# Gated mix of two Fourier filters: the hand-written order list in another arrangement

## Chip, cores and metric

The kernel runs on one core of a Trainium2 chip. The metric is the device time of one execution in microseconds, as the median of the runs. The engines are PE (matmul), DVE (vector), ACT (scalar), POOL (GpSimd) and SP, which issues nearly all transfers.

## The reference

```python
def filt(x, w_r, w_i):                                # x: (1, 2048, 1024) bf16
    X = rfft2(x.astype(float32), axes=(-2, -1)) * (w_r + 1j * w_i)
    return irfft2(X, s=(2048, 1024), axes=(-2, -1)).astype(bfloat16)

x = A_x
g = sigmoid((x * gate_w).sum(-1, keepdims=True))      # one gate value per row
out = g * filt(x, A_w_r, A_w_i) + (1 - g) * filt(x, B_w_r, B_w_i)
```

`B_x` isn't used. Both filters act on the same x, so the forward transform is done once; the two products with the weights and the two inverse transforms share most of their work, and the gate enters where the last step along the rows mixes the two halves.

## The kernel before

The transforms are matmuls with constant matrices (DFT factors). The 2048 rows are taken as 16 x 128 (index s = 0 to 15 for the factor of 16), and the 1024 columns are folded into even and odd frequencies. No loop orders the work: every step is a short code in one long string, `ORDER`, and the codes are called one after the other. A code's fields are its indices, then a PSUM bank (the last digit, for matmul codes) or an engine letter (A = ACT, D = DVE, P = POOL, S = SP). Each engine runs its own instructions strictly in the order in which the list names them, and waits, by semaphores that the framework derives from the tiles, for what others must have finished. So the list decides three things: the order on each engine and on SP's transfer queue, which engine does a copy or a sum, and which PSUM bank a matmul writes (a bank is free again when its reader has copied it out).

The codes that the texts below speak of, with the lines that the profile shows (copies by ACT and DVE all go through one helper, line 201 or 203):

| code | what it does | engine, line |
|---|---|---|
| `x:S:s:n`, `c:S:name`, `W:S:n` | load n slices of x, a constant, the weights of unit n | SP, L249, L254/L261, L273 |
| `F1:s:e`, `F1:s:o` | first matmul stage, even or odd part of slice s (8 matmuls) | PE, L336 |
| `FC`, `FX` | copy one half, or all, of an F1 result from PSUM to SBUF | ACT or DVE |
| `FD`, `FP` | fold it: a sum and a difference | DVE or POOL, L422 |
| `neg`, `pw` | prepare constants for F3 and for the patch | POOL |
| `F2:n:t`, `F3:n` | second and third stage for unit n (0 to 7 even frequencies, 8 to 15 odd) | PE, L528, L569 |
| `T:n:t`, `X:n` | copies of their results | ACT or DVE |
| `P:n` | product of X with the weights, 128 x 4096 | DVE, L586 |
| `Y:n`, `NA:n`, `N:n` | patch of the first column for even units | PE, DVE, POOL |
| `GH`, `GC`, `Gt`, `GK`, `GZ`, `GS` | gate values: matmuls, copies, sigmoid | PE, ACT, DVE |
| `GA:b`, `GB:b` | gate folded into the constants EA and EB, four slices from b | POOL or DVE, L515, L519 |
| `J:n`, `R:n:t` | first inverse stage of unit n (32 matmuls), and its two evictions | PE L632; ACT or DVE |
| `H:n:t` | store an eviction to a scratch tensor in DRAM (256 KB) | SP, L654 |
| `L:0:v`, `L:1:v` | read back row pair v, even or odd half (512 KB) | SP, L665 |
| `V:h:v:s`, `VC` | inverse along the 128 rows, row s of pair v, with EA and EB; its copy | PE, L675; ACT or DVE |
| `C:h:v:s`, `U:1:v:s` | last inverse stage, folded (4 matmuls of 256 columns) or full (4 of 512) | PE, L712, L703 |
| `E`, `EX`, `EQ`, `ES`, `EF` | even part: copies, then sum and difference, kept in SBUF as EV | ACT, DVE, POOL |
| `Ks`, `Kf`, `OK`, `QD`, `QP`, `OC`, `OP`, `OR` | odd part added to and subtracted from EV | ACT, DVE, POOL |
| `S:S:v` | store row pair v of the output | SP, L862 |

The stages overlap. In the profiled execution, F1 runs from 4.6 to 20 us, units 1 to 15 follow each other until 77 us on F2, F3, P, J and R, the even read-backs and V:0, C:0 run beside them from 57 us on, and the odd half V:1, C:1, U:1 and the output are last. A read-back of a half can be issued only when every store of that half has landed, since each pair holds rows of all units. The odd stores end with `H:15:0`; behind it on SP's queue stand `L:0:3` and the eight `L:1:v`.

Buffers: eight PSUM banks; two T, X and V tiles each, three product tiles, five eviction tiles that the output tiles share; eight slots of temporaries in `wx`, which also holds the weights of units 8 to 11.

```python
    def gate_a(e, b):
        s = slice(int(b), int(b) + 4)
        Q[e].tensor_tensor(C["EA"][:, s], C["EA"][:, s], bc(C["E"][:]).to_broadcast([P, 4, 128]), ALU.mult)
    ...
    order = [tok.split(":") for tok in ORDER.split()]
    for t in order:
        fn[t[0]](*t[1:])
```

Of the kernel before, what the change touches and what calls it, by code (L numbers as in the profile page):

```python
# [21 lines left out]


ORDER = """
warm:8 c:A:F1 x:S:0:1 x:S:1:1 F1:0:o:0 F1:0:e:4 F1:1:e:5 c:A:gws x:S:2:2 F1:1:o:2 F1:2:e:3 F1:3:e:6 tab:A FC:1:e:A FX:0:o:A
gc:P FX:1:o:A x:S:4:2 FC:0:e:D F1:3:o:2 FP:0:o FC:2:e:A FD:0:e FD:1:e x:S:6:2 F1:2:o:0 FC:3:e:A F1:5:e:5 F1:4:e:7 F1:4:o:1
x:S:8:2 FD:2:e FD:3:e x:S:10:2 x:S:12:2 FX:3:o:A x:S:14:2 FC:5:e:A c:S:E c:S:EZ c:S:WF:0:4 c:S:FD:0:1 FD:5:e FC:4:e:A c:S:w0
c:S:WF:4:16 FP:1:o FX:4:o:A FD:4:e F1:7:e:4 c:S:WJ:0:4 c:S:PM FC:7:e:A F1:6:e:3 W:S:1 F1:5:o:6 F1:9:o:7 FD:7:e FC:6:e:A
FX:2:o:A F1:9:e:2 F1:7:o:0 FP:3:o F1:8:e:4 FD:6:e FC:9:o:A FD:9:o F1:11:e:3 FX:5:o:A FP:4:o FC:9:e:A FC:8:e:A FD:9:e FP:2:o
FX:7:o:A FC:11:e:A F1:8:o:6 FD:8:e F1:10:e:7 c:S:FD:1:2 FD:11:e FP:5:o FC:10:e:A W:S:0 W:S:2 F1:12:e:1 FD:10:e FP:7:o  # L30
F1:15:e:0 neg:P:0:4 FC:15:e:A FD:15:e F1:14:e:2 F1:13:e:3 neg:P:4:16 FC:14:e:A FC:12:e:A FD:14:e F1:6:o:7 FC:13:e:A FC:8:o:A
F1:14:o:4 F1:15:o:0 F1:13:o:5 FD:13:e FD:12:e FX:6:o:A FD:8:o FC:15:o:A FC:14:o:A FD:14:o F1:11:o:7 F1:10:o:3 F2:1:0:1
F1:12:o:2 F2:1:1:6 FC:13:o:A FC:11:o:A F2:0:1:4 FC:10:o:A T:1:0:A F2:0:0:1 FC:12:o:A FD:11:o T:1:1:A FD:12:o T:0:1:A FD:10:o
T:0:0:A F3:1:6 X:1:A FP:6:o F2:2:1:4 FD:15:o pw:P F3:0:1 F2:4:1:0 F2:2:0:6 FD:13:o X:0:A P:1:b T:2:0:A T:2:1:A F2:3:1:5 Y:1:7
F2:3:0:2 Y:0:6 F2:4:0:1 T:3:1:A NA:1:D W:S:6 W:S:3 F3:2:3 W:S:7 W:S:4 c:S:WJ:4:16 W:S:10 W:S:8 P:0:b T:3:0:A X:2:A T:4:1:A
N:1:P GH:5 T:4:0:A GC:A F3:3:3 W:S:9 NA:0:D J:1:6:0 W:S:11 Gt:5 X:3:A R:1:0:A F2:5:1:2 P:2:b N:0:P GK:D Y:3:3 F2:5:0:4
R:1:1:A T:5:1:D Y:2:5 F3:4:6 F2:7:1:2 T:5:0:A NA:3:D NA:2:D P:3:b N:3:P N:2:P F2:7:0:3 J:0:0:4 T:7:1:D X:4:A c:S:IG T:7:0:A
R:0:1:D R:0:0:A J:3:2:6 R:3:1:A GZ:0:0 F3:5:4 GS:0 R:3:0:D F2:6:0:7 X:5:A J:2:0:2 T:6:0:A GZ:1:5 Y:4:4 F2:6:1:7 R:2:0:A W:S:5
P:4:b R:2:1:D H:0:0 H:1:0 H:1:1 NA:4:D P:5:b H:0:1 H:3:0 GS:1 T:6:1:A Y:5:0 F3:7:1 F2:8:1:3 X:7:A GA:P:0 F2:8:0:5 H:3:1
F2:9:1:4 F3:6:6 T:8:1:A T:8:0:A N:4:P X:6:A H:2:1 NA:5:D W:S:13 J:4:2:0 R:4:0:A F2:9:0:5 N:5:P Y:7:6 P:7:b R:4:1:A NA:7:D  # L40
T:9:0:D J:5:2:6 T:9:1:A R:5:0:A P:6:b R:5:1:A F2:10:0:5 Y:6:4 NA:6:D F2:10:1:0 F3:8:1 N:6:P T:10:0:D F3:9:3 N:7:P GB:P:0
X:8:A T:10:1:D P:8:b J:7:6:0 X:9:A R:7:1:A J:6:2:4 R:6:0:D F2:11:1:0 F2:12:1:1 W:S:12 W:S:15 H:2:0 H:4:1 H:5:0 H:5:1 H:4:0
P:9:b R:6:1:A R:7:0:A H:7:1 T:11:1:A F2:11:0:4 F3:10:2 T:11:0:A F2:12:0:0 H:6:1 X:10:A T:12:1:A F3:11:4 H:7:0 F2:13:1:7
F2:13:0:6 H:6:0 W:S:14 X:11:A L:0:1 T:13:0:A T:13:1:A T:12:0:D J:8:0:2 R:8:1:A F3:12:4 F2:14:0:6 F2:14:1:7 T:14:0:A R:8:0:A
GA:D:12 P:10:b X:12:D J:9:2:4 L:0:0 L:0:2 T:14:1:A J:10:0:6 P:11:b R:9:0:A F3:14:2 R:10:1:A GA:P:4 R:10:0:A R:9:1:D GB:P:12
J:11:4:6 P:12:b V:0:0:1:0 X:14:A V:0:0:0:3 V:0:1:0:1 VC:0:0:1:D R:11:0:A GA:P:8 GB:P:4 VC:0:0:0:A F3:13:2 R:11:1:A L:0:6
L:0:5 H:8:1 VC:0:1:0:D H:8:0 X:13:A J:12:0:4 GB:D:8 P:14:b H:9:1 F2:15:0:6 C:0:0:0:2 H:9:0 H:10:0 R:12:1:A E:0:0:D L:0:7
L:0:4 T:15:0:A H:10:1 F2:15:1:5 H:11:1 H:12:1 V:0:1:1:4 R:12:0:A T:15:1:A J:14:2:6 F3:15:0 VC:0:1:1:A R:14:1:A V:0:2:1:4
C:0:0:1:5 P:13:b R:14:0:D V:0:2:0:6 X:15:A J:13:0:2 E:0:1:A C:0:1:1:5 VC:0:2:0:A H:11:0 VC:0:2:1:A R:13:0:A P:15:b C:0:2:1:4
EX:2:1:D J:15:0:6 H:14:1 C:0:2:0:4 H:14:0 H:12:0 R:13:1:A EX:1:1:D R:15:1:A EX:2:0:A V:0:6:1:2 R:15:0:D H:13:0 H:13:1  # L50
C:0:1:0:3 V:0:6:0:5 V:0:4:0:4 EX:1:0:A VC:0:6:0:A V:0:4:1:0 VC:0:6:1:D V:0:5:1:7 H:15:1 VC:0:4:0:D VC:0:4:1:D H:15:0
EQ:2:0:1:D C:0:6:0:1 L:0:3 C:0:6:1:5 L:1:3 L:1:1 C:0:4:1:3 L:1:0 V:0:5:0:0 VC:0:5:1:D E:6:0:A E:6:1:A EQ:2:1:0:P EQ:1:0:0:D
ES:4:1:D EQ:1:1:1:P L:1:4 L:1:6 L:1:5 L:1:2 EQ:1:1:0:P VC:0:5:0:A V:0:7:0:6 C:0:4:0:1 C:0:5:1:7 EF:4:1 C:0:5:0:4 VC:0:7:0:A
ES:4:0:A V:0:7:1:5 C:0:7:0:3 ES:5:1:D V:0:3:1:0 ES:5:0:A EQ:2:1:1:P EQ:1:0:1:P L:1:7 EF:5:1 EF:4:0 EQ:2:0:0:P VC:0:7:1:A
EF:5:0 V:0:3:0:6 VC:0:3:1:A EX:7:0:A C:0:7:1:5 C:0:3:1:0 VC:0:3:0:D EX:7:1:A V:1:3:0:4 VC:1:3:0:A C:0:3:0:7 EQ:7:1:1:P
EQ:7:1:0:P V:1:3:1:6 ES:3:0:A EQ:7:0:1:P C:1:3:0:2 EQ:7:0:0:D V:1:1:0:3 ES:3:1:D EF:3:1 EF:3:0 V:1:0:0:7 Ks:3:0:A VC:1:3:1:A
C:1:3:1:6 VC:1:0:0:A Kf:3:0 OK:3:0:1:D Ks:3:1:A V:1:0:1:0 VC:1:1:0:A V:1:1:1:7 VC:1:0:1:A C:1:0:0:4 VC:1:1:1:A Kf:3:1
# [869 lines left out]
```

## Time and profile before

| | |
|---|---|
| three runs | 112.89, 113.46, 113.68 us; median 113.46 |
| profiled execution | 113.79 us, of which the span from the first to the last instruction is 112.0 |
| granted PE clock | 0.994 of full speed |
| busy | PE 98.0 us (88%), DVE 98.9 (88%), ACT 85.9 (77%), POOL 64.6 (58%) |
| transfers | 36.79 MB, mean 328 GB/s |
| DVE groups | P 18.2 + 9.8 us and four more, FD 16.4, OR 9.9 |
| chain that ended last | PE 40%, DMA 26%, DVE 14%, ACT 7%, issue 5% |

The shares are averages over the whole span. The engines are full for different reasons in different stages, so what a move is worth is read from the stage in which it lies: which engine or transfer is waited for there.

### The profile page before, as it was taken

Reading aid. Unit: us, or ns where it says so; the run is one execution under the profiler, and the core shown is the slowest. Engines: PE = TensorE matmul, PEld = TensorE weight load, DVE = VectorE, ACT = ScalarE, POOL = GpSimd, SP = SyncE. Lnnn points to the kernel's source line nnn. Section 1 sums busy time; section 2 is a strip of 40 time slices with the busy share of each in tenths; the row PEclk is TensorE's granted clock in tenths of the full one; section 3 lists DMA queues with packets and bytes.
Section 4 is the critical chain, followed back from the end, with each engine's and each line's share of the span. In section 5 each row is a group of like instructions: output and inputs, shape, how many; then the busy total and the mean of one; then the engine's idle time right before and its main releaser. Section 6 shows DMA issues by size and latency. Waiting matters only on the chain.

```text
span 112.0 us, 3830 instructions
## 1 busy us (share of the span) xinstructions
PE 98.0 (88%) x1559; PEld 69.6 (62%) x1559; DVE 98.9 (88%) x151; ACT 85.9 (77%) x141; POOL 64.6 (58%) x77
## 2 busy tenths in 40 slices
PE   5979999999996899879998599998999689999910
PEld 2569999775563475446554266656999577856500
DVE  0068999999999999999999999999799949999980
ACT  4167869999996999998999999998687667534500
POOL 3169999935901489188099600006700769999940
PEclk9999999999999999999999999999999999999997
DMA  3999999999999997996989999999879999409795
GB/s 64 353 335 405 399 359 338 335 415 419 400 408 418 379 366 251 357 364 235 298 237 350 312 335 380 409 375 373 272 212 367 336 385 379 198 37 402 282 401 198
DMA packets 17794, 36.79 MB, mean 328 GB/s; under 512 B 1904, under 2 KB 10736, under 8 KB 17776
## 3 DMA queue, kind: packets, MB, share of 16 engines
q1 hardware_dynamic: 17488, 36.44, 90.1%
q8 instruction: 12, 0.20, 0.7%
q10 hardware_dynamic: 288, 0.10, 0.3%
q14 instruction: 6, 0.05, 0.1%
HBM read 23.96 MB, written 12.58 MB: 326 GB/s over the span
## 4 chain that ended last, share of the span: by engine, by line
PE 40%; DMA 26%; DVE 14%; ACT 7%; issue 5%; POOL 2%; SPq 2%; DVEq 1%; POOLq 0%; ACTq 0%
PE ps L336 11%; DMA sc<-rl 9%; DVE p L586 7%; PE ps L703 7%; PE ps L528 6%; DMA ro<-sc 6%; DMA re<-sc 6%; PE ps L675 5%; DMA re<-in_x_dram 5%; ACT rl L201 4%; DVE rl L203 3%; PE ps L569 3%; PE ps L632 3%; POOL ea L515 2%; DVE ot L841 2%
## 5 line engine op out<-in xcount | busy, mean ns | idle before, releaser
L201 ACT CAST rl<-ps 128x1024 bf16<-128x1024 f32 x25 | 25.4, 1063 | 2.1 <-PE ps L632 2.1
L632 PE MATMUL ps<-p,wj 32*64 32x512 bf16 x512 | 17.8, 380 | 4.7 <-DVE rl L203 1.6
L201 ACT COPY wx<-ps 128x256 f32<-128x256 f32 (+1 forms) x42 | 17.1, 451 | 6.3 <-PE ps L336 4.5
L201 ACT CAST V<-ps 128x512 bf16<-128x512 f32 x25 | 14.4, 602 | 8.6 <-PE ps L675 7.7
L586 DVE TENSOR_TENSOR p<-X,ro 128x4096 bf16<-128x4096 bf16 x8 | 18.2, 2279 | 0.0
L528 PE MATMUL ps<-fd,y 128*128 128x256 bf16 x128 | 17.3, 273 | 0.7 <-ACT T L201 0.3
L422 DVE TENSOR_TENSOR y<-ps,wx 128x256 bf16<-128x256 f32 x48 | 16.4, 414 | 1.4 <-ACT wx L201 1.3
L806 POOL TENSOR_TENSOR re<-wx 128x256 f32<-128x256 f32 x9 | 6.3, 729 | 19.1 <-DVE wx L203 13.0
L201 ACT CAST X<-ps 128x1024 bf16<-128x1024 f32 x15 | 15.7, 1056 | 0.1
L336 PE MATMUL ps<-f,re 128*128 128x128 bf16 x256 | 15.1, 220 | 0.7 <-DMA re<-in_x_dram 0.7
L336 PEld LDWEIGHTS <-re 128*128 128x128 bf16 x256 | 14.7, 99 | 1.6 <-DMA re<-in_x_dram 1.1
L201 ACT CAST T<-ps 128x512 bf16<-128x512 f32 x26 | 15.3, 637 | 0.1
L615 POOL TENSOR_TENSOR p<-np 128x16 bf16<-128x16 f32 x8 | 9.8, 1251 | 9.6 <-DVE np L609 6.4
L632 PEld LDWEIGHTS <-wj 32*64 32x64 bf16 x512 | 8.4, 103 | 10.6 <-issue 5.9
L528 PEld LDWEIGHTS <-y 128*128 128x128 bf16 x128 | 11.2, 97 | 5.1 <-issue 4.0
L712 PE MATMUL ps<-ig,V 128*128 128x256 bf16 x88 | 12.3, 273 | 0.0
L422 POOL TENSOR_TENSOR y<-wx 128x256 bf16<-128x256 f32 x16 | 11.1, 732 | 1.1 <-ACT wx L201 1.0
L569 PE MATMUL ps<-T,wf 64*64 64x256 bf16 (+1 forms) x128 | 10.6, 333 | 0.0
L841 DVE TENSOR_TENSOR ot<-re,ps 128x512 bf16<-128x512 f32 x16 | 9.9, 675 | 0.0
L586 DVE TENSOR_TENSOR p<-X,wx 128x4096 bf16<-128x4096 bf16 x4 | 9.8, 2462 | 0.0
L675 PEld LDWEIGHTS <-ro 128*128 128x128 bf16 x128 | 8.1, 98 | 2.7 <-DMA ro<-sc 1.6
L675 PE MATMUL ps<-ea,ro 128*128 128x128 bf16 x64 | 8.4, 219 | 1.4 <-DMA ro<-sc 1.4
(70 smaller groups left out, 173.1 us busy)
## 6 DMA issues: line engine op xcount, KB each, us to landing
sc<-rl SPq DMA_DIRECT2D x32, 256.0 KB, 5.3
ro<-in_we_dram SPq DMA_DIRECT2D x8, 512.0 KB, 8.3
re<-sc SPq DMA_DIRECT2D x8, 512.0 KB, 6.7
ro<-sc SPq DMA_DIRECT2D x8, 512.0 KB, 7.7
re<-in_x_dram SPq DMA_DIRECT2D x7, 512.0 KB, 8.1
out_dram<-ot SPq DMA_DIRECT2D x7, 512.0 KB, 3.1
wx<-in_wo_dram SPq DMA_DIRECT2D x4, 512.0 KB, 9.7
y<-in_wo_dram SPq DMA_DIRECT2D x4, 512.0 KB, 5.2
```

Source lines behind the costliest of these rows:

```text
L201: nc.scalar.copy(out=out, in_=in_)
L336: nc.tensor.matmul(o, lhsT=lh, rhs=rh, start=(h == 0), stop=(h == 1))
L422: Q[e].tensor_tensor(yo[:, v, k:k + n, s1, :], a.rearrange("p (k c) -> p k c", c=4), b.rearrange("p (k c) -> p k c", c=4), op)
L528: nc.tensor.matmul(ps[:, v * 256:v * 256 + 256], lhsT=y[:, v, par, b, 2 * t:2 * t + 2, :, :].rearrange("p j s c -> p (j s c)"), rhs=C["FD" ...
L569: nc.tensor.matmul(view(ps[ho, tt * 512:(tt + 1) * 512], dst), lhsT=lh, rhs=view(T[hp(jh), tt, :], src), start=(w == 0), stop=(w == 1))
L586: nc.vector.tensor_tensor(p[:], xb, wb, ALU.mult)
L615: Q[e].tensor_tensor(Ps[n][:].rearrange("p r t w m -> p (r t w) m")[:, :, 0], t[:, :, 0], t[:, :, 1], ALU.add)
L632: nc.tensor.matmul(o, lhsT=lh, rhs=src[r, ri, wi, tt], start=(q == 0), stop=(q == 3))
L675: nc.tensor.matmul(ps[:, ch * 128:ch * 128 + 128], lhsT=RR[par][:, v, ch // 2, s, c0 + 256 * ab:c0 + 256 * ab + 128], rhs=Ew[:, s1, :], st ...
L703: nc.tensor.matmul(ps, lhsT=Vs[par, v][:, s, ch, :], rhs=rh, start=(ch == 0), stop=(ch == 3))
L712: nc.tensor.matmul(ps[:, o:o + 256], lhsT=Vs[par, v][:, s, ch, :], rhs=g[:, o:o + 256], start=(ch % 2 == 0), stop=(ch % 2 == 1))
L841: nc.vector.tensor_tensor(otile(v)[:, s, h, :], EV[:, v, s], PS["O", 1, v, s], (ALU.add, ALU.subtract)[h])
```

## The change

Only `ORDER` changes; the set of matmuls, transfers and products is the same, and every function stays as it was. By engine:

- DVE: it gets `FX:0:o`, `FC:1:e` and `FC:3:e` from ACT at the start; `T:7:0` instead of `T:5:1`; `GB:4` instead of `GA:12` and `GB:8`; `R:13:1`, `EX:1:0` and `EX:7:0` instead of `EX:2:1` and `EX:1:1`; and in the even and odd sums, several single operations change between ACT, DVE and POOL.
- POOL: the gate products run `GA:4`, then `GA:8`, `GA:0`, `GB:8`, `GB:0`, `GA:12`, `GB:12`; `neg:P:4:16` comes after `pw`.
- SP: the constants E, EZ, WF, w0 and PM change places among the loads of x and W; the order of the weights is other; of the even read-backs, `L:0:7` moves ahead and `L:0:6`, `L:0:5` behind some stores; the odd read-backs run 3, 0, 6, 1, 4, 7, 5, 2 instead of 3, 1, 0, 4, 6, 5, 2, 7.
- PE: `F1:12:o` comes ahead of `F2:1:0`; `V:1:0` and one half of `V:1:6` come ahead of `V:1:1`; the rest of the list shifts by a place or two; most PSUM banks are other ones.

The diff, cut to the lines that matter most:

```diff
-warm:8 c:A:F1 x:S:0:1 x:S:1:1 F1:0:o:0 F1:0:e:4 F1:1:e:5 c:A:gws x:S:2:2 F1:1:o:2 F1:2:e:3 F1:3:e:6 tab:A FC:1:e:A FX:0:o:A
+warm:8 c:A:F1 x:S:0:1 x:S:1:1 F1:0:e:2 F1:0:o:1 F1:1:e:7 c:A:gws x:S:2:2 tab:A F1:1:o:6 x:S:4:2 x:S:6:2 FX:0:o:D FC:0:e:D
+FC:1:e:D FX:1:o:A FD:0:e FD:1:e gc:P x:S:8:2 c:S:EZ F1:3:e:1 FP:0:o F1:3:o:6 F1:2:e:4 F1:2:o:5 x:S:10:2 c:S:WF:0:4 c:S:w0
+FP:1:o FX:3:o:A x:S:12:2 x:S:14:2 FC:3:e:D FD:3:e F1:5:e:2 F1:4:e:6 FC:2:e:A FX:2:o:A FC:5:e:A FC:4:e:A F1:4:o:0 c:S:FD:0:1
...
-T:9:0:D J:5:2:6 T:9:1:A R:5:0:A P:6:b R:5:1:A F2:10:0:5 Y:6:4 NA:6:D F2:10:1:0 F3:8:1 N:6:P T:10:0:D F3:9:3 N:7:P GB:P:0
+J:5:2:6 P:6:b T:9:1:A F2:10:0:5 Y:6:4 NA:6:D N:7:P N:6:P GA:P:8 GB:D:4 R:4:1:A R:5:0:A GA:P:0 GB:P:8 GB:P:0 F2:10:1:0 F3:8:1
+R:5:1:A X:8:A W:S:13 W:S:15 H:2:0 F3:9:3 T:10:1:D H:4:0 T:10:0:D J:7:6:0 X:9:A R:7:1:A R:7:0:A P:8:b J:6:2:4 F2:12:0:1
+F2:11:1:0 F2:11:0:6 R:6:0:D H:4:1 H:5:0 F3:10:2 GA:P:12 H:5:1 H:7:1 R:6:1:A T:11:1:A T:11:0:A H:7:0 F2:13:1:5 F2:12:1:4 H:6:0
...
-C:0:0:1:5 P:13:b R:14:0:D V:0:2:0:6 X:15:A J:13:0:2 E:0:1:A C:0:1:1:5 VC:0:2:0:A H:11:0 VC:0:2:1:A R:13:0:A P:15:b C:0:2:1:4
-EX:2:1:D J:15:0:6 H:14:1 C:0:2:0:4 H:14:0 H:12:0 R:13:1:A EX:1:1:D R:15:1:A EX:2:0:A V:0:6:1:2 R:15:0:D H:13:0 H:13:1
+H:10:0 H:10:1 L:0:4 L:0:6 L:0:5 VC:0:2:1:A E:0:1:A GB:P:12 J:13:0:2 P:15:b R:13:0:A R:13:1:D C:0:1:1:5 EX:1:1:A C:0:2:1:4
+J:15:0:6 EX:2:1:A R:15:0:D C:0:1:0:5 V:0:4:1:2 R:15:1:A VC:0:4:1:A H:12:1 H:11:1 H:12:0 V:0:4:0:4 C:0:2:0:3 VC:0:4:0:A
...
-EQ:2:0:1:D C:0:6:0:1 L:0:3 C:0:6:1:5 L:1:3 L:1:1 C:0:4:1:3 L:1:0 V:0:5:0:0 VC:0:5:1:D E:6:0:A E:6:1:A EQ:2:1:0:P EQ:1:0:0:D
-ES:4:1:D EQ:1:1:1:P L:1:4 L:1:6 L:1:5 L:1:2 EQ:1:1:0:P VC:0:5:0:A V:0:7:0:6 C:0:4:0:1 C:0:5:1:7 EF:4:1 C:0:5:0:4 VC:0:7:0:A
+L:1:3 L:1:0 L:1:6 L:1:1 L:1:4 L:1:7 C:0:5:0:3 ES:5:1:A VC:0:7:1:A C:0:6:0:0 V:0:7:0:4 EQ:1:1:1:P EQ:1:1:0:P C:0:6:1:7 E:6:0:A
+C:0:7:1:6 EQ:2:0:0:P EF:4:0 EQ:1:0:1:P EQ:2:1:1:D EF:5:1 VC:0:7:0:D L:1:5 L:1:2 ES:5:0:A E:6:1:A EQ:2:0:1:P V:0:3:0:2
...
-EQ:7:1:0:P V:1:3:1:6 ES:3:0:A EQ:7:0:1:P C:1:3:0:2 EQ:7:0:0:D V:1:1:0:3 ES:3:1:D EF:3:1 EF:3:0 V:1:0:0:7 Ks:3:0:A VC:1:3:1:A
-C:1:3:1:6 VC:1:0:0:A Kf:3:0 OK:3:0:1:D Ks:3:1:A V:1:0:1:0 VC:1:1:0:A V:1:1:1:7 VC:1:0:1:A C:1:0:0:4 VC:1:1:1:A Kf:3:1
+EQ:7:1:0:P EQ:7:1:1:P C:0:3:1:1 ES:3:0:D EF:3:0 V:1:0:0:5 VC:1:3:1:A C:1:3:1:0 Ks:3:0:A ES:3:1:A V:1:0:1:2 VC:1:0:0:A
+Ks:3:1:A C:1:0:0:7 V:1:6:1:4 Kf:3:0 VC:1:0:1:A EF:3:1 Kf:3:1 C:1:0:1:2 V:1:1:0:0 V:1:1:1:6 V:1:6:0:5 VC:1:1:0:A QD:0:0:0
...
-VC:1:2:1:A U:1:5:0:5 U:1:2:1:4 U:1:2:0:1 V:1:4:0:3 V:1:4:1:2 OR:5:1:0 QD:6:0:1 S:S:0 OP:1:0:1 OR:5:0:1 OR:5:0:0 S:S:1
+U:1:5:0:1 OR:5:0:0 VC:1:2:1:A U:1:5:1:0 VC:1:2:0:A OR:5:0:1 U:1:2:1:5 OR:5:1:0 OR:5:1:1 V:1:4:0:1 VC:1:4:0:A U:1:2:0:7
```

## The prediction, as it stood before the changed kernel ran

> **What bounds the kernel now.** I read four views in this order: the busy line of the page, the chain of waits, the timelines of DVE and POOL from 47 to 64 us, and the list of waits. The page first.
>
> ```profile
> PE 98.0 (88%) x1559; PEld 69.6 (62%) x1559; DVE 98.9 (88%) x151; ACT 85.9 (77%) x141; POOL 64.6 (58%) x77
> DMA  3999999999999997996989999999879999409795
> ```
>
> Nothing is idle: PE and DVE both stand at 88%, and the transfer engines are full in nearly every slice up to 95 us. So a reordered list can win only where one of these three waits for another, and the chain shows where (start, length, what):
>
> ```profile
> 77.05 0.96 DVE rl L203
> 78.01 0.18 issue
> 78.19 0.35 DVE V L203
> 78.54 3.59 DMA sc<-rl
> ...
> 83.19 6.73 DMA ro<-sc
> 89.91 0.05 issue
> 89.96 0.62 PE ps L675 x8
> ...
> 107.61 1.20 DVE ot L841 x2
> ```
>
> Up to 78 us the chain runs through DVE, which the timeline shows without a gap above 0.3 us from 10.2 us on. Its last eviction R:15:0 (77.05) lets store H:15:0 go (78.54, landed 82.13), all eight odd read-backs L:1:* wait for that landing, and PE stops at 88.6 until the third of them, L:1:0, lands at 89.91. From there PE runs without a break to 106.83 and DVE, after one wait of 1.38 us at 90.17, to 108.81. The list of waits has both:
>
> ```profile
> PE ps L675 <- DMA ro<-sc: 1.4, 1, 1.4
> DVE wx L833 <- ACT wx L201: 1.4, 1, 1.4
> ```
>
> The landings of the eight read-backs (issue plus time to landing, asked issue by issue) are 85.98, 87.21, 89.91, 91.21, 93.35, 94.62, 95.86 and 97.11: 1.25 us apart, but for two steps of 2.70 and 2.14.
>
> **The change, part by part.**
>
> *First stage, to P:1.* DVE gets a copy of 128x512 (0.60 start to start) and two of 128x256 (0.40 each) from ACT. Its work before P:1 is then 0.60 + 3x0.40 + 24 folds of 0.665 = 17.76; from the same start, 5.82, that is 23.6, and I add 0.1 for waits: P:1 at 23.7, against 23.99. The copies are paid by idle time: 0.73, 0.37 and 0.24 us of waiting before folds. The floor is X:1, ended at 23.58. Five constants move among the x loads on SP's queue; the 224 KB ahead of the last two x loads cost 0.56 at 1.27 us for 512 KB, but those tiles are now used at 16.3 us and later, and they landed at 13.66 and 15.51. On PE, F1:12:o goes ahead of F2:1:0 and fills the 0.3 us by which the last even fold is later. Gain 0.3 (bounds 0 and 0.4).
>
> *From P:1 to P:8.* T:5:1 goes to ACT and T:7:0 to DVE, one for one. Of DVE's two small gaps, 0.19 before R:3:0 and 0.26 before T:10:0, the second is filled by GB:4 (0.34), moved up from 66.96. ACT, full from 36 to 50 us, starts this stretch earlier too. I take P:8 at 49.1 instead of 49.48: gain 0.4 with the stage before.
>
> *Gate products on POOL.* GA:12 (0.34, start to start) leaves DVE and GB:4 leaves POOL, so that POOL now holds GA:8, GA:0, GB:8, GB:0, GA:12, GB:12 in one run, and none waits for DVE any more. Before, POOL sat idle for 3.40 us until GA:12 was done on DVE. These are the rows of DVE, then of POOL (start, length):
>
> ```profile
> 49.48 2.28 DVE L586 TENSOR_TENSOR p<-X,wx 128x4096 bf16<-128x4096 bf16 x1
> 51.68 1.22 DVE L203 CAST rl<-ps 128x1024 bf16<-128x1024 f32 x1
> 52.81 2.28 DVE L586 TENSOR_TENSOR p<-X,wx 128x4096 bf16<-128x4096 bf16 x1
> 59.50 3.01 DVE L586 TENSOR_TENSOR p<-X,wx 128x4096 bf16<-128x4096 bf16 x1
> ```
> ```profile
> 49.55 3.23 POOL L515 TENSOR_TENSOR ea<-ea,e 128x512 bf16<-128x512 bf16 x1
> 56.17 3.07 POOL L519 TENSOR_TENSOR eb<-e,ea 128x512 bf16<-128x512 bf16 x1 [3.40 <-DVE ea L515]
> 59.20 1.16 POOL L515 TENSOR_TENSOR ea<-ea,e 128x512 bf16<-128x512 bf16 x1
> ```
>
> A POOL product that meets a DVE product (P:n) finishes 1.0 us after it (52.77 after 51.76; 59.24 after 58.23). And where POOL had begun first, at 59.20 during a copy, P:11, begun at 59.50, took 3.01 instead of 2.28: it stood still for 0.73 until POOL was done. This happened once before, because POOL had no second product ready at the other places. Now it has. With P:8 from 49.1 to 51.3, GA:0 is done at 52.4 and GB:8 starts there; P:9 is due at 52.45 and waits until 53.35: 0.9. GB:0 starts when P:9 ends, runs 1.05, and T:12:0 covers 0.60 of that: P:10 waits 0.45. GA:12 starts when P:10 ends, X:12 (1.2) covers it, and GB:12 starts 0.25 ahead of P:11: 0.75. In all 2.1 against 0.73: loss 1.37. The case of P:10, a POOL product that starts right at the end of a DVE one with another DVE product soon behind, is in no row: bounds 0 and 1.05, and I take the overlap. For the three together the bounds are 0 (DVE always first: a gain of 0.73) and 3.5.
>
> The Trainium skill (SBUF — State Buffer, Who interferes with whom) says that VectorE and GpSimd share one port pair as an exclusive lock which whoever starts first keeps for the whole instruction, and that a VectorE instruction with two SBUF inputs takes part in this. By that rule P:10 waits its 0.45 like the others; by the row of P:11 alone it is open, and the sum would be 0.45 lower. The 3.01 row agrees with the rule.
>
> *To R:15:0.* P:11 ends at -0.4 - 0.34 + 1.37 = +0.6 against before. R:9:1, J:11, R:11:0 follow it directly, and then ACT runs without a gap from 64.8 to X:15 (ended 73.45; P:15 began at 73.48). So ACT carries the 0.6 to P:15, and the departure of GB:8 from DVE (0.34 at 66.96) does nothing. Behind P:15, EX:2:1 and EX:1:1 leave DVE (1.27) and R:13:1 comes (1.14); both fit into the 1.07 + 0.1 of J:15, for which R:15:0 waits. ACT takes the two copies ahead of R:15:1 while J:15 runs. R:15:0: 77.65, +0.6 (bounds -0.8, ACT's own gaps from 50 on plus the earlier start, and +2.5).
>
> *To the read-backs.* H:15:0 took 3.59 from issue to landing, 1.07 of it in the issue itself behind a full queue; an output store with a free queue takes 2.3. A later store finds less ahead of it, so between 0 and all of the 0.6 arrives; I take 0.4. The other moves on SP's queue (L:0:7 ahead, L:0:6 and L:0:5 behind, H:10:1 up) keep the same bytes between the same two ends, and V:0:4 to V:0:6, which use them from 77.9 on, find them landed by 75.
>
> *The tail.* L:1:0 becomes the second read-back (87.21 by slot) and L:1:6 the third, so V:1:0 finds its data and both 1.4 us waits shrink to 0.3. But pair 5 is now seventh and pair 2 eighth, and PE still takes 5 and 2 ahead of 4 and 7. V:1:5 comes due at 95.2 and waits for 95.86; V:1:2 is due at 96.8 and waits for 97.11. Behind that stand the same matmul groups as before: six of V at 0.44 and eight of U at 0.866 = 9.6, PE's end at 106.75 against 106.83. What was won at 89.9 is waited for at 95 to 97. DVE has 1.2 us less to catch up, and runs dry at 98.5 until U:1:5:0 is done at 99.05; its last 16 sums from there, at 0.605 plus 0.1, end at 108.9 against 108.81. Of OK and QP as many run on DVE as before. Tail: +0.1 (bounds -1.4, if the read-backs land faster, and +0.3).
>
> **Sum.** 0.4 + 0.1 = +0.5. The profiled execution took 113.79 (span 112.0 and 1.8 around it), 0.33 above the median of the three runs, 113.46. It would become 114.3, and the median 114.0.
>
> **Rivals.** (a) *The ports don't meet*: DVE's products always start first. Then P:11 also loses its old 0.73; R:15:0 comes 0.8 earlier, where ACT stops it, of which 0.5 reaches the read-backs, less 0.1 in the tail: 113.1. For it: P:8 (49.48) began 0.1 us before a POOL product ended and shows no delay. Against it: the 3.01.
> (b) *The ports meet in full* (the slower side): GA:0 starts just ahead of P:8 (49.1) as well, and P:9, P:10 and P:11 each wait out a whole POOL product: 0.9 + 3x1.05 = 4.0 in place of 0.73, less 0.74: +2.5 at R:15:0, about 2.0 at the read-backs: 115.5. It decides once the stalls pass 3 us in all. For it: POOL's run starts within 0.1 us of P:8 by my own times. Against it: R:6:0 and X:12 cover most of one product each.
> (c) *The new order of read-backs pays*: the two long steps between landings (1.45 and 0.9 above 1.25) do not come back or come late, the eighth lands near 95.7, and the 1.4 us wait of PE goes for good: 112.1. For it: six of eight steps were 1.25. Against it: the read-backs of the even half had such steps too, five landings from 61.30 to 68.84.
> (d) *The reordering does not take the wait away*: if 2.70 is the price of pair 0 and not of the third place, L:1:0 lands at 88.7 and V:1:1, fourth, at 92.1, later than before; the eighth stays. Nothing changes but small moves: 113.5.
>
> **How the numbers follow.** Forecast 0.42 (own range 113.3 to 114.9), (a) 0.16, (b) 0.22, (c) 0.16, (d) 0.04. About 1%, 1.1 us, can be told from no change here. Faster by more than that: 0.13 of (c) and 0.05 of (a), 0.18. Slower: 0.20 of (b) and 0.08 of the forecast, 0.28. Within 1%: 0.54. The range from 112.1 to 115.5 leaves out half of (c) and a little over a third of (b).
>
> **What would show it.** Right: products P:9, P:10, P:11 with 3.1, 2.7 and 3.0 us while POOL's gate products run without idle time from 48 to 61; R:15:0 at 77.4 to 78; no wait at V:1:0; PE waits ahead of V:1:5 and V:1:2; the end of PE 9.6 us after the last read-back lands. Wrong: all products at 2.28 (then (a)); the eighth read-back landing before 96 with PE unbroken to the end (then (c)); DVE late already at P:8; or a wait in the first 24 us that I took for hidden.

## The result, and the profile after

The changed kernel takes 114.41 us (median of 12 runs) against 113.20 for the kernel before in the same session: 1.011 times as long, 95% interval 1.008 to 1.013. In a later session it was 1.015 (1.011 to 1.019). The forecast was 114.0 from 113.46, that is +0.5; the change costs about 1.2. Ratios here and below leave out disturbed runs; medians hold all runs.

The profiled execution took 114.75 us, span 113.0. First the lines of its page, then of its chain of waits (start, length, what), then of its list of waits:

```profile
PE 99.8 (88%) x1559; PEld 70.7 (63%) x1559; DVE 99.9 (88%) x150; ACT 85.7 (76%) x141; POOL 65.1 (58%) x78
...
DMA  3999999999999799998999999999967999536985
```
```profile
79.85 4.32 DMA sc<-rl
...
87.67 10.40 DMA ro<-sc
98.07 0.05 issue
98.12 1.07 PE ps L675 x16
...
108.73 1.20 DVE ot L841 x2
```
```profile
PE ps L632 <- DVE rl L203: 1.9, 1, 1.9
...
PE ps L675 <- DMA ro<-sc: 0.8, 2, 0.7
```

The busy shares are those of before to within a point. The last store of the odd half, H:15:0, went at 79.85 and landed at 84.17, 2.04 us later than before. The read-back that the chain ends on is now the last one, which lands at 98.07; behind it PE works 9.8 us. The wait of 1.4 us at V:1:0 is gone; what is left for the odd read-backs is 0.67 for the first of them and 0.17 ahead of V:1:2. New is a wait of 1.9 us of PE for an eviction by DVE at 65 us. The reason for it is the timeline of DVE (start, length), and below it that of POOL:

```profile
49.70 2.28 DVE L586 TENSOR_TENSOR p<-X,wx 128x4096 bf16<-128x4096 bf16 x1
...
53.04 3.23 DVE L586 TENSOR_TENSOR p<-X,wx 128x4096 bf16<-128x4096 bf16 x1
56.19 0.68 DVE L203 CAST T<-ps 128x512 bf16<-128x512 f32 x1
56.79 2.64 DVE L586 TENSOR_TENSOR p<-X,wx 128x4096 bf16<-128x4096 bf16 x1
59.56 1.23 DVE L203 CAST X<-ps 128x1024 bf16<-128x1024 f32 x1
60.70 3.12 DVE L586 TENSOR_TENSOR p<-X,wx 128x4096 bf16<-128x4096 bf16 x1
```
```profile
48.62 4.38 POOL L515 TENSOR_TENSOR ea<-ea,e 128x512 bf16<-128x512 bf16 x2
52.96 4.32 POOL L519 TENSOR_TENSOR eb<-e,ea 128x512 bf16<-128x512 bf16 x2
57.24 3.20 POOL L515 TENSOR_TENSOR ea<-ea,e 128x512 bf16<-128x512 bf16 x1
60.52 1.16 POOL L519 TENSOR_TENSOR eb<-e,ea 128x512 bf16<-128x512 bf16 x1
```

P:9, P:10 and P:11 took 3.23, 2.64 and 3.12 instead of 2.28: 2.15 us of standing still, each time behind a POOL gate product that had begun ahead of them. POOL's run has no gap above 0.1 us.

Between the two profiles the end of DVE moved by 1.11 us (108.81 to 109.92). By the forecast's own steps:

| stretch | forecast | this pair of profiles |
|---|---|---|
| start of P:8 | -0.4 (49.1) | +0.22 (49.70) |
| P:8 to R:15:0 | +1.0 | +1.09 (28.66 instead of 27.57) |
| R:15:0 to landing of H:15:0 | -0.2 | +0.73 (5.81 instead of 5.08) |
| that landing to the eighth odd read-back | 0 | -1.08 (13.90 instead of 14.98) |
| eighth read-back to the end of DVE | +0.1 | +0.15 |

Three rows fail, and two of them nearly cancel. So the experiments ask three questions. Theory A: the port stalls are the price of this change. Theory B: SP's new queue delays the odd half. Theory C: the new list is slow in the first stage.

### The profile page after: what moved, and what is told of

It reads as the page before. It is cut to its first block, busy times and chain, and to the rows that moved or that the text cites. A ratio compares the mean times of both kernels' runs of the same rounds, so it can differ in the third digit from the quotient of the medians.

```text
span 113.0 us, 3837 instructions
## 1 busy us (share of the span) xinstructions
PE 99.8 (88%) x1559; PEld 70.7 (63%) x1559; DVE 99.9 (88%) x150; ACT 85.7 (76%) x141; POOL 65.1 (58%) x78
## 4 chain that ended last, share of the span: by engine, by line
DMA 45%; PE 20%; ACT 14%; DVE 6%; SPq 6%; issue 5%; DVEq 1%; ACTq 0%
DMA ro<-sc 9%; DMA sc<-rl 8%; DMA ro<-in_we_dram 7%; DMA wj<-cst_wj 7%; DMA wf<-cst_wf 7%; DMA re<-in_x_dram 7%; ACT rl L201 7%; PE ps L632 7%; PE ps L703 5%; ACT X L201 4%; PE ps L528 3%; SPq L665 3%; PE ps L675 3%; ACT T L201 2%; DVE p L586 2%
## 5 line engine op out<-in xcount | busy, mean ns | idle before, releaser
L201 ACT CAST rl<-ps 128x1024 bf16<-128x1024 f32 x24 | 24.2, 1049 | 2.9 <-PE ps L632 2.8
L632 PE MATMUL ps<-p,wj 32*64 32x512 bf16 x512 | 18.6, 380 | 5.0 <-DVE rl L203 1.9
L201 ACT CAST V<-ps 128x512 bf16<-128x512 f32 x28 | 15.6, 599 | 8.2 <-PE ps L675 6.2
L336 PEld LDWEIGHTS <-re 128*128 128x128 bf16 x256 | 15.5, 102 | 0.9 <-issue 0.6
L336 PE MATMUL ps<-f,re 128*128 128x128 bf16 x256 | 15.6, 226 | 0.2 <-ACT wx L201 0.2
L201 ACT CAST T<-ps 128x512 bf16<-128x512 f32 x26 | 14.6, 623 | 0.1
L515 POOL TENSOR_TENSOR ea<-ea,e 128x512 bf16<-128x512 bf16 x4 | 9.9, 2494 | 4.1 <-ACT ea L485 4.1
L586 DVE TENSOR_TENSOR p<-X,wx 128x4096 bf16<-128x4096 bf16 x4 | 11.3, 2816 | 0.0
L203 DVE COPY wx<-ps 128x256 f32<-128x256 f32 (+1 forms) x8 | 4.0, 520 | 7.9 <-PE ps L336 5.4
```

Of the source, the lines that this page charges most:

```text
L201: nc.scalar.copy(out=out, in_=in_)
L336: nc.tensor.matmul(o, lhsT=lh, rhs=rh, start=(h == 0), stop=(h == 1))
L586: nc.vector.tensor_tensor(p[:], xb, wb, ALU.mult)
L632: nc.tensor.matmul(o, lhsT=lh, rhs=src[r, ri, wi, tt], start=(q == 0), stop=(q == 3))
```

## The experiments

All ratios are to the kernel before, run beside them. "Stalls" are what the products P:8 to P:15 took above 2.28 us.

**1. The changed kernel again.** No edit.

> The changed kernel itself once more, to see what varies from one execution to the next. Theory A (the first-stage step of the forecast was right, the late PE clock hid it): the moment at which the first matmuls go from 107 to 56 ns apart is again another one, and P:1 follows it: near 23.5 with a switch before 5.2 us, near 24.1 with one after 6 us; P:8 near 49.05 or 49.7. Theory C (the new list is slow in the first stage): P:1 at 24.0 or later whatever the switch does. In both, P:9, P:10 and P:11 stand still 0.94, 0.35 and 0.84 us as in the four executions seen so far, and the median is 1.0 to 1.2 us above before.

Ratio 1.015 (1.011 to 1.019), 1.7 us where 1.0 to 1.2 were expected. Stalls 0.94, 0.36 and 0.84, P:8 at 49.70 with a switch at 6.9 us. Both theories' figures for P:1 lie close together here (24.14), so what decides is the table over all profiles. These are the first matmuls of F1 on PE's timeline (start, length, count), of the kernel before, of the changed kernel, and of the changed kernel in experiment 6 (whose first stage is the same):

```profile
4.57 2.11 PE L336 MATMUL ps<-f,re 128*128 128x128 bf16 x32
```
```profile
4.56 3.38 PE L336 MATMUL ps<-f,re 128*128 128x128 bf16 x40
```
```profile
4.57 2.64 PE L336 MATMUL ps<-f,re 128*128 128x128 bf16 x40
```

That is 66, 84 and 66 ns a matmul. In the records one follows another after 107 ns at first and after 56 from a certain moment on. This moment was at 4.9, 6.6 and 5.0 us in these three. The windows view shows a granted clock of 1.00 ahead of it too, but the trace holds no record of the clock before that moment: its first record, of full clock, begins at 4.90, 6.61 and 4.97 us. So the switch is one of PE's clock. Over all profiles in which the third load of x had landed by 7.4 us and the warm-up was the same:

| first stage of | moment of the switch, us | P:1 begins, us |
|---|---|---|
| before | 4.9, 5.3, 5.4 | 23.99, 23.92, 24.13 |
| before | 5.9, 6.5 | 24.50, 24.51 |
| changed | 5.0, 5.1 | 23.48, 23.56 |
| changed | 6.1, 6.6, 6.9 | 24.01, 24.14, 24.14 |

At like moments the changed list is 0.4 to 0.5 us ahead. The moment belongs to the execution and not to the list, and it is worth 0.5 to 0.6 us. The pair of profiles compared an early execution of before with a late one of after. Theory C falls. In three more profiles (experiments 8 and 11, and 10 with three of the copies back on ACT) the third load of x landed only at 7.8 to 8.2, and P:1 began at 24.35 to 24.46 whatever the clock did.

The Trainium skill (TensorE: Matmul & The Clock Gate, What's actually happening) describes such a switch: PE's clock is gated to half until it has been busy for a window of 3.4 us, and the windows run freely. The first matmul started at 1.18 in every profile, and in the thirteen with the full warm-up the switch came 3.4 to 5.7 us later, so the trace agrees with the rule, though the spread is wider than the half microsecond to either side that the page states.

**2. A late clock by force.** The changed kernel with a short warm-up.

```diff
-warm:8
+warm:2
```

> The changed kernel with 2 matmuls of warm-up instead of 8 and nothing else: PE stands idle from 2.0 to about 4 us. Theory A (the moment of the switch from 107 to 56 ns sets P:1): the switch follows the busy time of PE, so it comes 2 to 4 us later than in the other profiles, at 7.5 to 11 us; F1's first 30 to 60 matmuls take twice their time, and P:1 moves to 25 to 27; median 115.5 to 118. Rival (the pace of the first matmuls follows something else, the landing of x or of the constants): the switch at 4.6 to 7 us as before, P:1 at 23.5 to 24.2, median as the changed kernel's.

The switch came at 7.45 us, but P:1 at 24.21, only 0.07 later than with a switch at 6.6. The size was wrong: PE began F1 at 4.29 instead of 4.57, because the warm-up no longer stood in front of it, and only some 30 matmuls paid, (7.45 - 4.29)/0.107. What P:1 follows is the end of F1:1:o: 6.71, 7.24, 7.50, 7.63 and 7.74 us go with 23.48, 24.01, 24.14, 24.14 and 24.21. The ratio of 1.020 (1.013 to 1.028, four runs) came out as theory A of this run said, but not for its reason: the profile shows another loss, at 65 us, which has a heading of its own below.

**3. The gate products of the changed kernel, placed as before.**

```diff
-GA:P:4 ... GA:P:8 GB:D:4 ... GA:P:0 GB:P:8 GB:P:0 ... GA:P:12 ... GB:P:12
+GA:P:0 ... GB:P:0 GA:P:4 ... GA:D:12 GB:P:12 GA:P:8 GB:P:4 P:10:b ... GB:D:8 P:14:b
```

> The changed kernel with one part undone: the gate products are placed as before (POOL: GA:0, GB:0, GA:4, GB:12, GA:8, GB:4; DVE: GA:12 and GB:8). Theory A (the port stalls cost the time): P:9 and P:10 fall to 2.3 us, only P:11 keeps about 0.7 us of waiting, so the three products stand still 0.7 us in all instead of 2.15; GA:12 costs DVE 0.34 again; R:15:0 comes 0.8 to 1.1 us earlier after P:8 than in the changed kernel, and 0.5 to 0.9 us of it reaches the end: median 113.5 to 113.9. Theory B (the late landing of H:15:0 is a matter of the transfer queue, the products only fill time that is there anyway): the products shrink, but H:15:0 lands as late as in the changed kernel, 84 us, and the median stays at 114.2 to 114.6. Theory C (the first stage is the loss): P:8 stays late and the median stays above 114.2 as well. On PE, the first matmuls of F1 come 107 ns apart and later ones 56; the moment of the switch was 4.9 us in the profile before and 6.6 in the profile after. If this moment is the execution's own and not the list's, it will be some third value here.

Ratio 1.007 (1.003 to 1.011), median 114.4. Theory A's sum did not come: P:9 and P:10 were free as it said, P:11 stood still 0.72, but now P:8 stood still 0.93. The two rows, of DVE's and of POOL's timeline:

```profile
49.57 3.21 DVE L586 TENSOR_TENSOR p<-X,wx 128x4096 bf16<-128x4096 bf16 x1
```
```profile
49.48 1.16 POOL L515 TENSOR_TENSOR ea<-ea,e 128x512 bf16<-128x512 bf16 x1
```

In the kernel before the same pair stood the other way round, P:8 at 49.48 and POOL's product at 49.55, and there POOL took 3.23 us and P:8 2.28. A lead of 0.1 us decides which of the two waits. The run shows the mechanism, but it does not measure the price, since 1.65 us of stalls were left.

**4. The placing of the changed kernel, in the kernel before.**

```diff
-GA:P:0 ... GB:P:0 ... GA:D:12 P:10:b ... GA:P:4 ... GB:P:12 ... GA:P:8 GB:P:4 ... GB:D:8
+GA:P:4 ... NA:6:D GB:D:4 ... N:7:P GA:P:8 GA:P:0 GB:P:8 GB:P:0 GA:P:12 GB:P:12
```

> The kernel before with one part of the change alone: POOL's gate products in one unbroken run (GA:4, then GA:8, GA:0, GB:8, GB:0, GA:12, GB:12), GB:4 on DVE, GA:12 and GB:8 off DVE. Theory A (port stalls): two or three of P:8 to P:12 take 2.6 to 3.3 us and stand still 1.5 to 2.5 us in all instead of 0.73; R:15:0 comes 0.6 to 1.2 us later than the 77.05 before; median 113.8 to 114.4. Theory B (ACT and the transfer queue set the end of this stage): the products grow, but R:15:0 and H:15:0 stay within 0.3 us, median 113.0 to 113.5.

Ratio 1.009 (1.005 to 1.013), median 114.27. P:9, P:10 and P:11 on DVE's timeline:

```profile
53.43 3.22 DVE L586 TENSOR_TENSOR p<-X,wx 128x4096 bf16<-128x4096 bf16 x1
...
57.17 2.63 DVE L586 TENSOR_TENSOR p<-X,wx 128x4096 bf16<-128x4096 bf16 x1
...
61.07 3.12 DVE L586 TENSOR_TENSOR p<-X,wx 128x4096 bf16<-128x4096 bf16 x1
```

The same three stalls as in the changed kernel, to 0.01 us, in a list that differs everywhere else (P:8 adds 0.09); R:15:0 stands 28.73 behind P:8, 1.16 later than before. This placing alone brings most of the loss. Theory A holds.

**5. The placing taken out of the way.** The changed kernel, with POOL's products so placed that each starts during a product of DVE and runs in a long copy behind it.

```diff
-GA:P:8 GB:D:4 ... GA:P:0 GB:P:8 GB:P:0 ... GA:P:12 ... P:10:b ... P:13:b ... GB:P:12
+GA:P:0 GB:P:0 GB:D:4 ... GA:D:12 GB:P:12 P:10:b ... GA:D:8 GB:P:8 P:13:b
```

> The changed kernel with the gate products spread so that each POOL product starts during a DVE product and is due in a long PSUM copy behind it: POOL GA:4, GA:0, GB:0 as now, then GB:12 behind a GA:12 on DVE ahead of P:10, and GB:8 behind a GA:8 on DVE ahead of P:13; GB:4 on DVE as now. Theory A (port stalls): P:8 to P:15 all take 2.28 us, DVE pays 0.34 twice, so that P:12 starts 1.6 to 1.8 us earlier after P:8 than in the changed kernel (13.4 instead of 15.2) and R:15:0 1.0 to 1.5 us earlier, less where ACT holds it; with the transfer queue as it is, 0.4 to 1.0 us of that reaches the end: median 113.4 to 114.0. Theory B (transfer queue): R:15:0 comes earlier, H:15:0 lands at most 0.4 us earlier, median 114.1 to 114.5. If the rule of one start ahead of the other is wrong, some product stands still all the same, and P:12 moves less.

Ratio 0.995 (0.992 to 0.999), median 112.65: faster than the kernel before, and 1.5 to 2% faster than the changed one. P:9 to P:11 on DVE's timeline with the GA:12 between them, then GB:0 and GB:12 on POOL's:

```profile
52.45 2.28 DVE L586 TENSOR_TENSOR p<-X,wx 128x4096 bf16<-128x4096 bf16 x1
...
55.25 0.41 DVE L515 TENSOR_TENSOR ea<-ea,e 128x512 bf16<-128x512 bf16 x1
55.58 2.28 DVE L586 TENSOR_TENSOR p<-X,wx 128x4096 bf16<-128x4096 bf16 x1
...
59.14 2.28 DVE L586 TENSOR_TENSOR p<-X,wx 128x4096 bf16<-128x4096 bf16 x1
```
```profile
49.26 3.15 POOL L519 TENSOR_TENSOR eb<-e,ea 128x512 bf16<-128x512 bf16 x1
55.80 3.07 POOL L519 TENSOR_TENSOR eb<-e,ea 128x512 bf16<-128x512 bf16 x1 [3.39 <-DVE ea L515]
```

No product stands still; POOL's take 3.1 us instead, waiting out DVE's, which costs nothing. P:8 to P:12 takes 13.35 us instead of 15.18, R:15:0 comes 27.15 behind P:8 instead of 28.66. P:8 begins at 49.12, with a switch of the clock at 5.1: the 49.1 of the forecast. What reaches the end is more than the 0.4 to 1.0 us that was expected.

**6. The queue of before in the changed kernel.** Only SP's order of the even read-backs and of H:8 to H:15.

```diff
-L:0:1 L:0:0 L:0:2 L:0:7 H:8:0 H:8:1 H:9:1 H:9:0 H:10:0 H:10:1 L:0:4 L:0:6 L:0:5 H:12:1 ...
+L:0:1 L:0:0 L:0:2 L:0:6 L:0:5 H:8:1 H:8:0 H:9:1 H:9:0 H:10:0 L:0:7 L:0:4 H:10:1 H:11:1 ...
```

> The changed kernel with SP's queue of even read-backs and of the stores H:8 to H:15 in the order of the kernel before, nothing else. Theory B (the queue delays H:15:0): the landing of H:15:0 comes 3.5 to 3.7 us after its issue instead of 4.32, the eight odd read-backs 0.6 us earlier, median 113.8 to 114.0. Rival: the 4.32 us are an accident of one execution or of the state of the transfers, H:15:0 lands between 3.6 and 4.4 us after its issue here too, and the median stays at 114.2 to 114.6. A third way: even read-backs that now come earlier push the stores H:8 and H:9 behind them and nothing is won.

Ratio 1.004 (1.000 to 1.008), median 113.97: about 0.7 us under the changed kernel, though the intervals overlap. In the profile H:15:0 landed 2.94 us after its issue, but it was issued 2.33 after R:15:0 instead of 1.49, so that the landing came 5.27 behind R:15:0 instead of 5.81.

**7. The queue of the changed kernel in the one before.** The diff of experiment 6 the other way round, on the kernel before.

> The kernel before with SP's queue of even read-backs and of the stores H:8 to H:15 in the order of the changed kernel, nothing else. Theory B (the queue costs by itself): between the landings of the third even read-back and of H:15:0 the same 5.5 MB take 17.7 to 18.1 us, as in the three profiles with this order, instead of 16; H:15:0 lands 0.5 to 1.5 us later than 82.13 with R:15:0 unchanged at 77.0 to 77.6; median 113.6 to 114.3. Rival (the queue follows the evictions, its own order is free): landing of H:15:0 5.1 us behind R:15:0 as before, median 113.0 to 113.4.

Ratio 1.005 (1.001 to 1.008), median 113.68. The two runs agree on a price of half a microsecond or a little more for the new queue. The profile does not show where: H:15:0 landed 5.01 us behind R:15:0, as before, and what lay between was no slower (15.63 us from the landing of L:0:7, the fourth even read-back, against 15.87 from the fourth in the kernel before; the figures of the expectation too run from the fourth landing, not the third). Over all profiles but that of experiment 10 (an execution of 116.9 us, far above its median), this landing came 4.9 to 6.1 us behind R:15:0, with both queues at both ends of that range. One trace of it is in the windows view (stretch, its length, busy time of PE, PEld, DVE, ACT and POOL, granted clock, DMA share, GB/s), first of the kernel before, then of the changed one:

```profile
69.00:72.00 3.00, 2.85 (x62) 1.68 (x60) 3.00 (x3) 3.00 (x6) 0.00 (x0) 1.00 1.07 410
72.00:75.00 3.00, 2.82 (x57) 2.14 (x55) 3.00 (x3) 3.00 (x6) 0.00 (x0) 1.00 1.06 381
```
```profile
69.00:72.00 3.00, 2.89 (x58) 1.97 (x44) 2.85 (x3) 3.00 (x5) 0.00 (x0) 1.00 1.03 313
72.00:75.00 3.00, 2.82 (x64) 1.93 (x56) 2.94 (x3) 3.00 (x5) 0.00 (x0) 1.00 0.95 307
```

The transfer engines are full in both, and move a fifth to a quarter less in the changed kernel. Yet with the new queue and without stalls (experiment 5) it was 376 and 380 GB/s, and in experiment 7 378 and 370, while with the old queue and the stalls (experiment 6) it was 299 and 375. So the slow stretch is not the queue alone. How the queue loses its half microsecond stays open.

**8. The odd read-backs in order of use.**

```diff
-L:1:3 L:1:0 L:1:6 L:1:1 L:1:4 L:1:7 ... L:1:5 L:1:2
+L:1:3 L:1:0 L:1:6 L:1:1 L:1:5 L:1:2 ... L:1:4 L:1:7
```

> The changed kernel with the odd read-backs queued in the order in which PE uses them (3, 0, 6, 1, 5, 2, 4, 7). Theory A (the tail is bound by the eight landings and by DVE behind them, and the order of the last four costs only PE's short waits): the waits ahead of V:1:5 and V:1:2 (0.2 to 0.3 us together) go, DVE's one dry stretch of 0.25 us goes, PE's end comes within 9.5 us of the last landing or earlier, median 0 to 0.3 us below the changed kernel: 114.1 to 114.4. Rival C (the order pays): the waits were worth more, since each puts off a whole row of DVE work: 0.6 to 1.0 us below, 113.4 to 113.8.

Ratio 1.007 (1.004 to 1.011), between the two cases, and its interval overlaps that of the changed kernel: inconclusive as a time. PE ended 9.61 us behind the last landing instead of 9.81, the 0.2 that was expected. Its profiled execution lost 1.4 us at 65 us, of which more below. The eighth read-back landed 13.96 us behind H:15:0, as in the changed kernel (13.90).

**9. Pairs 1 and 0 exchanged, in the kernel before.**

```diff
-L:1:3 L:1:1 C:0:4:1:3 L:1:0
+L:1:3 L:1:0 C:0:4:1:3 L:1:1
```

> The kernel before with the odd read-backs of pairs 1 and 0 exchanged (3, 0, 1, 4, ...). If the long step at the third read-back (2.70 and 2.38 us in two profiles with the old order) belongs to the third place or to the state of the transfers, L:1:1 takes it here, L:1:0 lands 1.25 behind the first, PE's wait of 1.4 us at V:1:0 turns into one at V:1:1 two places earlier, median 113.0 to 113.4. If it belongs to the order (pair 1 ahead of pair 0), the step is 1.3, the eighth lands 14.0 instead of 15.0 us behind H:15:0, and the median falls to 112.4 to 112.8. With the old order and the new queue of even read-backs the step was 1.54, so the state of the transfers is the likelier.

Ratio 1.001 (0.997 to 1.005). The third landing was 2.63 us behind the second again, now with pair 1 in that place; PE waited 1.81 us for it, and the eighth came 15.25 behind H:15:0. So the long step belongs neither to pair 0 nor to the order of these two pairs. It came in three of the five profiles of lists built on the kernel before and in none of the nine built on the changed one, so something else in the list may favour it. What goes with it is the third issue on SP: it took 1.06, 0.83 and 1.33 us in the three profiles with a long third step, and 0.4 to 0.6 in the other eleven, two of which had the old order (experiments 7 and 12). Whether the long issue makes the step long or only goes with it was not tried.

The other long step is in every profile: one read-back, at 91 to 96 us, lands 2.1 to 2.7 us behind the one before it. In each trace's packet records a fetch of 16 KB of instructions, some 1.0 us long, begins at 89 to 94, 2.2 to 2.9 us ahead of that landing. That this fetch makes the step was not tried; the read-back is the fifth of the eight each time, so its place could matter as well.

**10. Three first-stage copies back on ACT**, in the kernel of experiment 5.

```diff
-FX:0:o:D FC:0:e:D FC:1:e:D ... FC:3:e:D
+FX:0:o:A FC:0:e:D FC:1:e:A ... FC:3:e:A
```

> The changed kernel with clean products, and the three copies FX:0:o, FC:1:e, FC:3:e back from DVE to ACT. If the 0.4 to 0.5 us by which the new list starts P:1 earlier (at the same moment of the PE clock's switch: 23.5 against 24.0 with a switch before 5.2 us, 24.0 to 24.15 against 24.5 after 5.9) come from these copies, P:1 falls back to 23.9 to 24.0 or 24.4 to 24.5 and the median is 0.2 to 0.5 above that of the clean kernel, ratio 0.998 to 1.000. If they come from the order of F1, folds and constants, P:1 stays at 23.5 to 23.6 or 24.0 to 24.15, or comes earlier by up to 0.5, and the ratio stays near 0.995.

Ratio 0.992 (0.988 to 0.996): no loss to be seen, which speaks for the order of F1, folds and constants as the source of the 0.4 us, and against the copies. Its P:1 can't be used (24.41, with the third load of x at 7.8), so this stays likely and no more.

**11. Experiments 5, 6 and 8 together.** The two lines on SP's queue, on the kernel of experiment 5:

```diff
-L:0:1 L:0:0 L:0:2 L:0:7 H:8:0 H:8:1 ... L:0:4 L:0:6 L:0:5 ... L:1:3 L:1:0 L:1:6 L:1:1 L:1:4 L:1:7 L:1:5 L:1:2
+L:0:1 L:0:0 L:0:2 L:0:6 L:0:5 H:8:1 H:8:0 ... L:0:7 L:0:4 ... L:1:3 L:1:0 L:1:6 L:1:1 L:1:5 L:1:2 L:1:4 L:1:7
```

> The changed kernel with the clean products of the run above, with the even read-backs and the stores H:8 to H:15 in the order of before on SP's queue, and the odd read-backs in the order of use. Both losses are taken away together: theory A and B add up, R:15:0 near 76.5 to 77.2, H:15:0 landed by 81 to 82, the eighth odd read-back 14.0 us behind it (not the 15.0 of the kernel before), at 95 to 96; median 112.0 to 112.8, below the kernel before by 0.5 to 1.2. If only one of the two is a cost of its own and the other is hidden behind it: 113.0 to 113.6.

Ratio 0.991 (0.988 to 0.994), median 112.35, the fastest kernel of the study: 0.9 us below the kernel before and 2.1 to 2.6 below the changed one. P:8 to P:12 takes 13.36 us, the eighth read-back lands 14.20 behind H:15:0, both as expected. The landing of H:15:0 at 83.13 was not: the profiled execution had the late load of x, and 6.07 us behind R:15:0.

**12. The clean placing in the kernel before.**

```diff
-GA:P:0 ... GB:P:0 ... GA:D:12 P:10:b ... GA:P:4 ... GB:P:12 ... GA:P:8 GB:P:4 ... GB:D:8
+GA:P:4 ... NA:6:D GB:D:4 ... N:7:P GA:P:0 GB:P:0 ... GA:D:12 GB:P:12 P:10:b ... GA:D:8 GB:P:8 P:13:b
```

> The kernel before with the clean placing of the gate products alone (POOL GA:4, GA:0, GB:0, then GB:12 behind GA:12 on DVE, GB:8 behind GA:8 on DVE; GB:4 on DVE in the gap ahead of T:10:0). Theory A (port stalls are a cost of their own, in this list too): P:11 loses its 0.72, DVE holds as many gate products as before (GA:12, GA:8 and GB:4 in place of GA:12 and GB:8, the third in a gap of 0.26), P:8 to P:12 takes 13.36 instead of 14.09, R:15:0 comes 27.15 behind P:8 instead of 27.57; 0.3 to 0.6 of it reaches the end: median 112.7 to 113.0, ratio 0.994 to 0.998. Rival (the good of the clean kernels came from meeting the changed list's other parts): no change, 113.2.

Ratio 0.996 (0.992 to 1.000), median 112.81, no stalls but 0.09 at P:8, R:15:0 27.14 behind P:8 (27.15 expected). In either list the placing of the gate products sets the time, and with the clean placing the two lists can't be told apart, so that the rest of the change nets to nothing:

| placing of the gate products | in the kernel before | in the changed one |
|---|---|---|
| as in the changed kernel (stalls 2.1 to 2.2) | 1.009 | 1.011, 1.015 |
| as before (0.7; with P:8 caught 1.65) | 1 | 1.007 |
| clean (0 to 0.1) | 0.996 | 0.995 |

## Why the prediction was right in direction, and short in size

*First stage, P:8 at 49.1.* Right at a like clock: 49.04 and 49.12 with an early switch. The 49.70 of the profile after is the late switch, which no profile of one execution could have foretold.

*The three port stalls, 2.1 us.* Right: 2.15, in this kernel and, to 0.01, in another list. The case that was in no row, P:10 behind a POOL product that starts as a product of DVE ends, came out at 0.36 against the 0.45 taken. In all profiles a product lost what was left of POOL's product when it began, less 0.13 us; that is why P:8 at 49.48, with 0.11 us left, shows no delay. By the Trainium skill's rule (SBUF — State Buffer, Who interferes with whom) whoever starts first keeps the ports for its whole instruction; the pairs at 49.5 us, 0.07 and 0.09 us apart and with opposite losers, agree with it. Rival (a), no meeting, is out; so is (b), since P:8 was not caught: GA:8 had only 0.07 us to go when P:8 began at 49.70, and the next POOL product, begun at 49.73, waited for it.

*P:8 to R:15:0, +1.0.* Right: 28.66 where 28.55 follows from the forecast. ACT also sets a floor, as it said: the clean placing won 1.83 us at P:12 and 1.51 at R:15:0.

*The rest of SP's queue at nothing.* This step failed. The sentence was that the other moves "keep the same bytes between the same two ends"; exchanging the queues is worth about 0.5 us in one kernel and 0.7 in the other by the runs, though the first interval begins near zero, those of the second pair overlap, and no profile shows the place. If that price is right, it makes up most of the 0.7 by which the forecast fell short. The sentence also named only some of the moves: the stores H:11, H:12 and H:14 change places among themselves too. "Between 0 and all of the 0.6 arrives" failed with it: in this pair 2.04 us arrived of 1.31. Equal bytes were taken for equal time, in a stretch where the transfer engines are full and their rate from 69 to 75 us ranges from 263 GB/s (experiment 1) to 410 in the profiles.

*The tail.* The waits went as the forecast said at V:1:0 (none) and V:1:2 (0.17), and PE's end came 9.81 us behind the last landing (9.6); at V:1:5, where 0.66 was forecast, none is to be seen. The step that failed is that both long steps between landings stay: one did not come back, and the eighth landed 1.08 earlier behind H:15:0. This is half of rival (c), but not for its reason, as the order of pairs 1 and 0 has no part in it (experiment 9). Rival (d) is out by the same run. That the pair of profiles still came to +1.11 is partly luck, since this gain and the late landing of H:15:0 nearly cancel.

*A loss that the forecast did not hold.* It stands under the last heading, since its share of the median could not be measured.

## What to carry to other kernels

Where POOL and DVE share work on SBUF, look at which of two instructions starts first, not at the sum of their times: a POOL product that starts 0.1 us ahead of a DVE product costs DVE 0.9 us, one that starts 0.1 us behind it costs nothing. Give POOL's instruction a reason to start late (here a short DVE instruction that it depends on, just ahead of the long one) and let it run beside a copy from PSUM. Before the stages of two profiles are compared, line them up by what differs from one execution to the next; here the first matmuls and the third load together moved P:1 by up to 1 us, as much as the effect that was looked for.

## What was not expected of the hardware

PE's clock can fall back to half in mid-kernel. In the profiles of experiments 2 and 8 the granted clock read 0.50 for some 3.4 us from 65.5 and 66 us on, and R:15:0 came 30.15 and 30.01 us behind P:8 instead of 28.66. These are PE's row with the wait ahead of it, and rows of the windows view (columns as above), both of experiment 2:

```profile
65.07 1.56 PE L632 MATMUL ps<-p,wj 32*64 32x512 bf16 x32 [1.91 <-DVE rl L203]
```
```profile
65.50:66.00 0.50, 0.50 (x23) 0.25 (x8) 0.50 (x1) 0.00 (x1) 0.00 (x0) 0.51 0.86 293
66.00:67.00 1.00, 1.00 (x21) 0.44 (x6) 1.00 (x1) 0.35 (x1) 0.00 (x0) 0.50 1.00 359
...
68.50:69.00 0.50, 0.50 (x8) 0.50 (x6) 0.00 (x0) 0.50 (x2) 0.00 (x0) 0.58 1.14 391
69.00:69.50 0.50, 0.50 (x15) 0.28 (x13) 0.28 (x1) 0.50 (x2) 0.00 (x0) 1.00 1.07 369
```

It follows the wait of 1.91 us that the late P:11 gives PE. By the trace's records of the clock the fall lasted 3.41 us both times, from 65.51 and from 66.01. From 62.0 to 65.4 PE was busy for 1.49 of 3.40 us, in the same way in the changed kernel's own profile, where the clock stayed up; with the clean placing it was 2.80 and the wait 0.87. The clock fell in two of the five profiles of the changed list with its own placing (the changed kernel, experiments 1, 2, 6 and 8), and in none of the others. So the stalls have a second price, about 1.4 us in some executions, which would help to explain why the clean placing gave more than its 1.5 us at R:15:0. How often it is paid was not measured; a hint is the mean granted clock of each run, 0.981 and 0.985 in these two profiles: such a mean, 0.985 or less, stands beside 11 of the 46 runs of these five kernels and beside 3 of 186 runs of the others.

The Trainium skill (TensorE: Matmul & The Clock Gate, What's actually happening) lets the clock fall back after an idle window of 3.4 us, and the windows run freely. The length at half clock fits one such window. The trace bears the free windows out: the falls come 17 and 18 times 3.413 us behind the switch at 7.48 and 4.57, and in the window that ended at each fall PE was busy for 1.50 us, with the whole gap inside it. In the three profiles where the clock stayed up the windows lay otherwise, and the one that held most of the gap had 1.59, 1.86 and 2.06 us of work (experiment 1, the changed kernel, experiment 6). So where the windows happen to lie decides whether the same row costs 1.4 us. The limit is not sharp, as a window with 1.50 us at 87 to 90 us of experiment 10 brought no fall. But PE was not idle for a whole window here: it was busy for 44% of 3.4 us, and its longest gap was 1.91. By this trace, then, the gap that is safe is shorter than the page's.
